# Copying the shifted values by halves of the heads, in other units, and loading the first half of the values earlier, in an attention-and-experts kernel

## The chip, the cores and the metric

The kernel runs on one core of a Trainium2 chip. A core has a matrix engine (TensorE, "PE" in the profile, with its weight loads as "PEld"), a vector engine (DVE), a scalar engine (ACT), GpSimd (POOL) and SyncE (SP), which here only issues transfers. Each engine works through its own list of instructions in order and waits on semaphores for the others. The metric is the device time of one execution in microseconds.

## The reference

Two blocks follow each other. The first is causal attention with a window of 64 positions over 8 batches, 8 heads, 576 positions and a head size of 64. The second sends each of the 4608 rows, 512 wide, to one of eight experts; a row may keep the expert of the row before it.

```python
scores = scale * np.matmul(q, k.transpose(0, 1, 3, 2))
mask = (rel >= 0) & (rel < window)          # rel = query position - key position
attn = softmax(np.where(mask, scores, -1e9))
x = np.matmul(attn, v)                      # (B, H, S, D) -> (B, S, H*D)
...
e = fresh_e if s == 0 or local_gate[b, s] < 0.5 else prev_e
h = np.maximum(x[b, s] @ w1[e], 0.0)
out[b, s] = p[e] * (h @ w2[e])
```

## The kernel before

The 4608 rows are cut into nine spans of 512 (`SC`), and the eight heads into four pairs. One span and one pair of heads, written (sc, hp) here, is a unit; there are 36 of them, and `attention` walks through them in order. For each unit `scores` (from L329) makes the transposed scores in PSUM on PE (L335), ACT takes the exponential (L351) and DVE multiplies with a 0/1 mask (L354). `values` (from L357) multiplies the result with the values on PE (L364); a column of ones beside the values gives the sum, DVE takes its reciprocal (L369) and scales the rows (L374). Scores run two units ahead of values (`LEAD`), so in the step of unit (sc, hp) PE makes first the scores of the unit two further on, and then the values of (sc, hp).

Keys are needed in blocks of 64. A query block in an even place uses the 64 keys of the block before it and its own, and these lie in other halves of the 128 partitions than for a query block in an odd place. So there are two copies of the values of a span: `va` as loaded, and `vb`, shifted by 64 positions: its lower 64 partitions are those of `va`, its upper 64 partitions are those of the chunk of 128 positions before. `shift(sc)` (from L306) makes `vb` of a span: the upper half by ACT in three copies (L311, L314, L318), the lower half by POOL in two (L312, L316). It is a generator; each `next` lets it issue the part up to the next `yield`. `shift_first` (from L320) does the same for span 0 by halves of the heads (POOL L326, ACT L327). There are three `va` and two `vb` buffers.

The steps in which the parts of `shift(sc + 1)` are issued are set at L414 to L417: for span 0 all four parts in unit (0, 3), for the later spans two parts in unit (sc, 0) and two in unit (sc, 1).

ACT, PE and SP take their instructions in the order in which the program text issues them (L179); DVE and POOL are ordered by a scheduler. What else stands in ACT's queue near the copies: for the spans 0 to 3, `turn` transposes the finished rows x of a span on PE, two pairs of heads at a time (L259), and ACT copies the result out of PSUM (L262). The first half of span sc is turned in unit (sc, 3), the second half in unit (sc + 1, 0). `gates(sc)` in unit (sc + 1, 1) multiplies this with the gate weights on PE (L273), and ACT copies the product out (L280, tile `gs`); in unit (sc + 1, 2) PE transposes `gs` (L285) and DVE sums it into the logits (L291). For the spans from 4 on, the logits come from the values directly: `gates(sc + 1)` in unit (sc, 2) (L275, L280), and `spread` in unit (sc, 3) puts them as extra columns beside `va` and `vb` (ACT L301 to L303, DVE L304). PSUM results of `values`, `turn`, `gates` and the router alternate between two banks (`bank`).

At the start SP loads in this order: keys and queries of pair 0, of pair 1, the first half of the heads' values, keys and queries of pairs 2 and 3, the second half of the values (L217; keys and queries come together, as `kq`). PE first runs 12 transposes of the identity (`warm`, L223), which compute nothing that is used, then the scores of the units (0, 0) and (0, 1), then 24 more such transposes, and then the values of (0, 0). DVE builds the second mask (L245, L248) after the mask product of (0, 1). The load of span 2 waits, by a tiny transfer on SP's queue (L213), for the first reciprocal.

After attention, `Experts` runs the experts' matrix products on the sorted rows (L1203, L1234, L1112, L1155), with weights loaded two jobs ahead into the buffers that keys and queries had.

Of the kernel before, what the change touches and what calls it, by code (L numbers as in the profile page):

```python
# [20 lines left out]
B, H, S, DH = 8, 8, 576, 64  # L21
# [3 lines left out]
WIN = 64  # L25
# [28 lines left out]
NSC = N // SC  # L54
# [95 lines left out]
def attention(ctx, tc, ring, kq, v3, v4, vt, vh, xs, lt, ok, wg, wg2, ident, rt, ex):  # L150
# [14 lines left out]
    nc = tc.nc  # L165
# [9 lines left out]
    def bank():  # L175
        ps_x.reverse()
        return ps_x[0].tile([P, 2, SC], F32, name="xo")
# [3 lines left out]
    kqs, qts, kts, vts, vas, vbs = {}, {}, {}, {}, {}, {}  # L181

    def width(sc):
        return VW if sc in GATED else VX

    def space(name, sc):
        return kp.tile([P, 4, H, width(sc)], F32, name=name, bufs=2 if name == "vb" else 3)

    def load(sc, parts):
        for part in parts:  # L190
            if part == "turned":
                t = tp.tile([P, HP * (SC + WIN)], F32, name="vtt")
                vts[sc] = main, ahead = t[:, :HP * SC], t[:, HP * SC:]
                nc.sync.dma_start(out=main, in_=vt[GATED.index(sc)].rearrange("p h x -> p (h x)"))
                if sc - 1 not in GATED:

                    nc.sync.dma_start(out=ahead, in_=vh.rearrange("p h x -> p (h x)"))
            elif isinstance(part, tuple):
                if sc not in vas:
                    vas[sc] = space("va", sc)  # L200
                src, h = v4[GATED.index(sc)] if sc in GATED else v3[sc], slice(*part)
                nc.sync.dma_start(out=vas[sc][:, :, h], in_=src[:, :, h])
            else:
                if sc not in kqs:
                    kqs[sc] = ring.tile([P, HP, 2, SC], F32, name="w")
                    kts[sc], qts[sc] = kqs[sc][:, :, 0], kqs[sc][:, :, 1]
                nc.sync.dma_start(out=kqs[sc][:, part], in_=kq[sc, :, part])
# [3 lines left out]
    def until(i, x):  # L211

        nc.sync.dma_start(out=late[:, i:i + 1], in_=x)  # L213

    pairs = slice(0, HP // 2), slice(HP // 2, HP)
    whole = (0, H)
    load(0, [slice(0, 1), slice(1, 2), (0, H // 2), pairs[1], (H // 2, H)])  # L217

    def warm(n):

        r = bank()
        for _ in range(n):
            nc.tensor.transpose(r[:, 0, :P], ident, ident)  # L223
# [16 lines left out]
    def build_mask(i):  # L240
        m = cp.tile([P, KB, 2, WIN], F32, name=f"mask{i}")
        for c in range(2):
            h = slice(c * WIN, (c + 1) * WIN)
            for par in range(2):
                nc.vector.tensor_scalar(m[h, :, par, :], colf[h], rowf[h], None, Alu.is_ge if par == c else Alu.is_lt)  # L245
        mid = MID[i]
        other = slice((1 - mid % 2) * WIN, (2 - mid % 2) * WIN)
        nc.vector.memset(m[other, mid // 2, mid % 2, :], 0.0)  # L248
        masks.append(m.rearrange("p a b q -> p (a b q)"))
# [38 lines left out]
    def logits(sc, gated):  # L288

        gt = back(*gated).rearrange("p (c h g) -> p c g h", c=4, h=HP)[:, :, :E + 1]  # L290
        nc.vector.tensor_reduce(lt[:, 4 * sc:4 * sc + 4, :], gt, axis=AX.X, op=Alu.add)  # L291
# [14 lines left out]
    def shift(sc):  # L306

        va = vas[sc]
        vb = vbs[sc] = space("vb", sc)
        w = slice(width(sc - 1))  # L310
        nc.scalar.copy(vb[WIN:, 0, :, w], vas[sc - 1][WIN:, 3])  # L311
        nc.gpsimd.tensor_copy(vb[:WIN, :2], va[:WIN, :2])  # L312
        yield
        nc.scalar.copy(vb[WIN:, 1:3], va[WIN:, :2])  # L314
        yield
        nc.gpsimd.tensor_copy(vb[:WIN, 2:], va[:WIN, 2:])  # L316
        yield
        nc.scalar.copy(vb[WIN:, 3], va[WIN:, 2])  # L318

    def shift_first(half):  # L320

        va, h = vas[0], slice(4 * half, 4 * half + 4)
        if not half:
            vbs[0] = space("vb", 0)
            nc.gpsimd.memset(vbs[0][WIN:, 0], 0.0)
        nc.gpsimd.tensor_copy(vbs[0][:WIN, :, h], va[:WIN, :, h])  # L326
        nc.scalar.copy(vbs[0][WIN:, 1:, h], va[WIN:, :3, h])  # L327

    def scores(sc, hp):  # L329
        qt, kt = qts[sc], kts[sc]  # L330
        sp = ps_s.tile([P, 2, SC], F32, name="sp")

        def one(j, c, kt, block, a, b):
            h = slice(j * DH, (j + 1) * DH)
            nc.tensor.matmul(sp[c * WIN:(c + 1) * WIN, j, a:b], lhsT=kt[h, hp, block * WIN:(block + 1) * WIN],  # L335
                             rhs=qt[h, hp, a:b], start=True, stop=True)

        for s in range(5):
            for c in range(2):
                for j in range(2):  # L340
                    if c == 0:
                        if s < 4:
                            one(j, 0, kt, 2 * s, s * P, (s + 1) * P)
                    elif s:
                        one(j, 1, kt, 2 * s - 1, s * P - WIN, min(s * P + WIN, SC))
                    elif sc:
                        one(j, 1, kts[sc - 1], KB - 1, 0, WIN)
                    else:
                        one(j, 1, kt, 1, 0, WIN)
        p = pp.tile([P, 2, SC], F32, name="p")  # L350
        nc.scalar.activation(p, sp, Act.Exp, scale=DH ** -0.5)  # L351
        a = 0 if sc == KB else (MID[sc % 2] - sc) * WIN
        m = masks[sc % 2][:, a:a + SC].rearrange("p (o x) -> p o x", o=1)
        masked.append(nc.vector.tensor_tensor(p, p, m.to_broadcast([P, 2, SC]), op=Alu.mult))  # L354
        return p
# [23 lines left out]
    masked = []  # L379
    for u in units[:LEAD]:  # L380
        ps[u] = scores(*u)
    shift_first(0)
    with tc.issue_after(masked[-1].ins):
        build_mask(1)
    warm(24)
    until(0, masks[0][:1, :1])
    load(1, [pairs[0], whole, pairs[1]])
    moves, gated, turned, old = (), None, None, None
# [17 lines left out]
    for i, (sc, hp) in enumerate(units):  # L406
        if hp == 0:
            x, g = wk.tile([P, 4, HP, 2, DH], F32, name="x"), None
            if sc in GATED:
                g = wk.tile([P, 4, HP, 2, E + 1], F32, name="g")  # L410

        if 1 < i < len(units) - LEAD:
            ps[units[i + LEAD]] = scores(*units[i + LEAD])
        if hp == (0 if sc else 3) and sc + 1 < NSC:  # L414
            moves = shift(sc + 1)
        for _ in range(2 if sc else 4):
            next(moves, None) if moves else None  # L417
        if hp == HP - 1:
            if sc + 1 in GATED:
                spread(sc + 1, gated)  # L420
            if sc not in GATED:
                turn(sc, x, 0)
                old = x
        elif sc and sc - 1 not in GATED:
            if hp == 0:
                turn(sc - 1, old, 1)
            elif hp == 1:
                turned = gates(sc - 1)
            else:
                logits(sc - 1, turned)  # L430

        if side is None and 4 * sc >= C1 and hp >= 2:
            side = rt.first(psum)
        step()
        values(sc, hp, ps.pop((sc, hp)), x, g)
        if i < 2:
            ps[units[i + LEAD]] = scores(*units[i + LEAD])
        if i == 0:
            shift_first(1)
            until(1, allr[:1, 0, 0, 0, :1])  # L440
            load(2, [pairs[0], whole, pairs[1]])
        if i == 2 * HP:
            with tc.issue_after(masked[-1].ins):
                rt.prepare()
        if hp == 2 and sc + 1 in GATED:
            gated = gates(sc + 1)
        if 0 < sc < NSC - 2 and hp in (0, 2):
            load(sc + 2, [pairs[1]] if hp else [whole, pairs[0]])
        if hp == 2 and sc + 2 in GATED:
            load(sc + 2, ["turned"])  # L450
        if (sc, hp) == (NSC - 3, 3):
            ex.jobs = [ex.weights({}, -1)]
            if side == ():
                ex.rows(ex.jobs[0], -1)
        if (sc, hp) == (NSC - 1, 0):
            ex.jobs.append(ex.weights({}, -2))
        step()
        if hp == HP - 1:
            if sc in GATED:
                nc.vector.tensor_reduce(lt[:, 4 * sc:4 * sc + 4, :], g.rearrange("p c h j e -> p c e (h j)"),  # L460
                                        axis=AX.X, op=Alu.add)
            nc.gpsimd.dma_start(out=xs[sc * SC:(sc + 1) * SC, :].rearrange("(c p) d -> p c d", p=P),
                                in_=x.rearrange("p c h j d -> p c (h j d)"))
# [899 lines left out]
```

## Time and profile before

| what | us |
|---|---|
| ten runs: median (lowest to highest) | 664.06 (662.17 to 668.14) |
| the profiled execution | 666.12 |
| its span, first to last instruction | 664.4 |
| PE busy in the span | 631.8 (95%) |
| DVE / ACT / POOL busy | 384.2 / 177.9 / 124.8 |
| matrix products of scores, L335 (72 instructions each for 36 pairs of weight load and product) | 44.8 |
| exponentials, ACT L351, 36 of them | 36.9 |

The page gives for each engine its busy time, and in its groups the idle time just before an instruction with what ended it ("<-"). "issue" there means that the instruction waited for nothing that the profile shows. A timeline line has the start, the duration, the engine, the line of the kernel, what is written from what, and in brackets the idle time before it.

### The profile page before, as it was taken

What the parts mean: (1) busy time and instruction counts of PE and PEld (TensorE: products, weight loads), DVE (VectorE), ACT (ScalarE), POOL (GpSimd) and SP (SyncE); (2) the same over time, 40 slices, a digit from 0 to 9 for tenths busy, and PEclk for the clock granted to TensorE, in tenths of its full rate; (3) what the DMA queues carried; (4) which work ended last, traced back from release to release, by engine and by line L of the source; (5) the groups of instructions that cost most, each with busy time, mean ns of one, the idle gap of its engine ahead of it and who ended that gap; (6) DMA issues with size and microseconds to landing.
All of it is one profiled execution on the core that took longest, in us unless ns stands there. A gap on an engine that the chain in (4) does not pass through costs nothing. (4 is left out here: it accounts for less than half of the span.)

```text
span 664.4 us, 15065 instructions
## 1 busy us (share of the span) xinstructions
PE 631.8 (95%) x6521; PEld 546.0 (82%) x6521; DVE 384.2 (58%) x693; ACT 177.9 (27%) x274; POOL 124.8 (19%) x128
## 2 busy tenths in 40 slices
PE   8889877989999999999999999999999999999995
PEld 7667665777777789989989998999799979997973
DVE  6665679773941168358628844863566366637310
ACT  3755645521211121203212130322131213211200
POOL 4411112311214101122113111311211120101011
PEclk9999989999999999999999999999999999999998
DMA  8989889999877967487459557755865586457540
GB/s 336 420 316 365 326 296 360 381 354 364 299 287 297 382 239 270 190 306 295 166 218 371 213 219 281 293 205 177 312 246 194 189 313 240 160 198 287 195 155 23
DMA packets 22479, 178.37 MB, mean 268 GB/s; under 512 B 3037, under 2 KB 4195, under 8 KB 11652
## 3 DMA queue, kind: packets, MB, share of 16 engines
q1 hardware_dynamic: 13588, 147.82, 59.0%
q0 software_dynamic: 8816, 29.50, 11.2%
q8 instruction: 53, 0.87, 0.5%
q14 instruction: 22, 0.18, 0.1%
HBM read 158.43 MB, written 19.40 MB: 268 GB/s over the span
## 5 line engine op out<-in xcount | busy, mean ns | idle before, releaser
L1185 POOL DMA_INDIRECT out_dram<-y,idx x36 | 39.8, 1106 | 301.6 <-DVE y L1164 142.1
L1203 PEld LDWEIGHTS hp<-xt,w 128*128 128x128 f32 (+1 forms) x1152 | 88.2, 168 | 3.4 <-issue 3.1
L1203 PE MATMUL hp<-xt,w 128*128 128x128 f32 (+1 forms) x1152 | 89.4, 252 | 0.0
L1112 PE MATMUL hp<-xs,ws 128*128 128x128 f32 x624 | 73.9, 275 | 0.0
L1112 PEld LDWEIGHTS hp<-xs,ws 128*128 128x128 f32 x624 | 71.8, 192 | 0.0
L1155 PE MATMUL hp<-ws,hs 128*128 128x256 f32 x312 | 71.6, 379 | 0.0
L1234 PE MATMUL yp<-w,h 128*128 128x512 f32 x160 | 70.9, 594 | 0.0
L1036 POOL DMA_INDIRECT xg<-xs,idx x40 | 46.2, 1156 | 114.6 <-PE tp L1061 84.1
L1155 PEld LDWEIGHTS hp<-ws,hs 128*128 128x128 f32 x312 | 59.3, 190 | 8.1
L354 DVE TENSOR_TENSOR p<-p,mask 128x1024 f32<-128x1024 f32 x36 | 46.1, 1286 | 22.6 <-ACT p L351 22.4
L1234 PEld LDWEIGHTS yp<-w,h 128*128 128x128 f32 x160 | 29.5, 190 | 32.6 <-issue 31.8
L1123 DVE TENSOR_TENSOR h<-hp,keep 128x512 f32<-128x512 f32 x39 | 26.9, 691 | 49.1 <-PE hp L1112 49.1
L364 PE MATMUL xo<-vb,p 128*64 128x74 f32 (+1 forms) x576 | 44.4, 229 | 9.2 <-DVE va L304 5.3
L364 PEld LDWEIGHTS xo<-vb,p 128*64 128x64 f32 x576 | 38.8, 138 | 17.2 <-issue 8.0
L1112 PEld LDWEIGHTS hp<-xt,w 128*128 128x128 f32 x416 | 49.3, 192 | 3.4 <-issue 2.4
L1112 PE MATMUL hp<-xt,w 128*128 128x128 f32 x416 | 51.0, 276 | 0.0
L1164 DVE SCALAR_TENSOR_TENSOR y<-hp,pw,kept 128x256 f32<-128x256 f32 x39 | 18.3, 481 | 56.2 <-issue 33.6
L351 ACT ACTIVATE p<-sp 128x1024 f32<-128x1024 f32 x36 | 36.9, 1026 | 47.9 <-PE sp L335 42.9
L1155 PE MATMUL hp<-w,h 128*128 128x256 f32 x208 | 49.5, 381 | 0.0
L335 PE MATMUL sp<-w 64*64 64x128 f32 (+1 forms) x1296 | 44.8, 278 | 3.3 <-issue 3.3
L335 PEld LDWEIGHTS sp<-w 64*64 64x64 f32 x1296 | 39.2, 143 | 10.5 <-issue 8.3
L364 PE MATMUL xo<-va,p 128*64 128x74 f32 (+1 forms) x576 | 44.5, 229 | 1.2 <-issue 1.2
(268 smaller groups left out, 898.8 us busy)
## 6 DMA issues: line engine op xcount, KB each, us to landing
w<-in_w_dram SPq DMA_DIRECT2D x54, 2048.0 KB, 8.7
w<-in_kq_dram SPq DMA_DIRECT2D x17, 1024.0 KB, 11.8
xs<-x POOLq DMA_DIRECT2D x9, 1024.0 KB, 12.0
va<-in_v_dram SPq DMA_DIRECT2D x5, 1184.0 KB, 5.4
vtt<-in_vt_dram SPq DMA_DIRECT2D x5, 1024.0 KB, 5.1
va<-in_v_dram SPq DMA_DIRECT2D x3, 1040.0 KB, 11.1
va<-in_v_dram SPq DMA_DIRECT2D x2, 520.0 KB, 7.9
w<-in_kq_dram SPq DMA_DIRECT2D x2, 512.0 KB, 4.0
```

Source lines behind the costliest of these rows:

```text
L335: nc.tensor.matmul(sp[c * WIN:(c + 1) * WIN, j, a:b], lhsT=kt[h, hp, block * WIN:(block + 1) * WIN], rhs=qt[h, hp, a:b], start=True, stop= ...
L351: nc.scalar.activation(p, sp, Act.Exp, scale=DH ** -0.5)
L354: masked.append(nc.vector.tensor_tensor(p, p, m.to_broadcast([P, 2, SC]), op=Alu.mult))
L364: nc.tensor.matmul(xo[par * WIN:(par + 1) * WIN, j, s * VW:s * VW + n], lhsT=p[:, j, b * WIN:(b + 1) * WIN], rhs=w[:, s, 2 * hp + j, :n], ...
L1036: self.nc.gpsimd.indirect_dma_start(out=x, out_offset=None, in_=self.xs[:rows, :], in_offset=bass.IndirectOffsetOnAxis(ap=idx[:, s:s + 1], ...
L1112: nc.tensor.matmul(out[:, m, :], lhsT=a[:, kk, m * P:(m + 1) * P], rhs=b[:, kk, :], start=start and m + kk == 0, stop=stop and (m, kk) == ...
L1123: nc.vector.tensor_tensor(o, x, y, op=add)
L1155: nc.tensor.matmul(out, lhsT=a[:, m, :], rhs=b[:, m, :], start=start and m == 0, stop=stop and m == FK // 2 - 1, skip_group_check=True)
L1164: nc.vector.scalar_tensor_tensor(y[i][:, j * w:(j + 1) * w], x, pw[i], y2, Alu.mult, Alu.add)
L1185: self.nc.gpsimd.indirect_dma_start(out=self.out[:, :], out_offset=bass.IndirectOffsetOnAxis(ap=st["idx"][:, s:s + 1], axis=0), in_=y, in_ ...
L1203: nc.tensor.matmul(hp[a, i, :], lhsT=st["w1"][:, kk, m * P:(m + 1) * P][:, a], rhs=st["xt"][:, kk, :n], start=(kk == 0), stop=(kk == DK - 1))
L1234: nc.tensor.matmul(yp, lhsT=st["h"][:, m, :P], rhs=st["w2"][:, m, :], start=(m == 0), stop=(m == FK - 1))
```

## The change

It has four parts. `shift` works by halves of the heads: a half is two ACT copies (one chunk from the span before, three chunks of the own span) and one POOL copy, and there are two halves. The halves of `shift(sc + 1)` are issued in units (sc, 1) and (sc, 2), those of `shift(1)` in (0, 3) and (1, 0). At the start the first half of the values is loaded ahead of the keys and queries of pair 1. `shift_first(0)` is issued between the scores of (0, 0) and those of (0, 1), and the second group of identity transposes has 4 instead of 24.

```diff
-    load(0, [slice(0, 1), slice(1, 2), (0, H // 2), pairs[1], (H // 2, H)])
+    load(0, [slice(0, 1), (0, H // 2), slice(1, 2), pairs[1], (H // 2, H)])
...
-        w = slice(width(sc - 1))
-        nc.scalar.copy(vb[WIN:, 0, :, w], vas[sc - 1][WIN:, 3])
-        nc.gpsimd.tensor_copy(vb[:WIN, :2], va[:WIN, :2])
-        yield
-        nc.scalar.copy(vb[WIN:, 1:3], va[WIN:, :2])
-        yield
-        nc.gpsimd.tensor_copy(vb[:WIN, 2:], va[:WIN, 2:])
-        yield
-        nc.scalar.copy(vb[WIN:, 3], va[WIN:, 2])
+        for half in range(2):
+            h = slice(4 * half, 4 * half + 4)
+            nc.scalar.copy(vb[WIN:, 0, h, :width(sc - 1)], vas[sc - 1][WIN:, 3, h])
+            nc.scalar.copy(vb[WIN:, 1:, h], va[WIN:, :3, h])
+            nc.gpsimd.tensor_copy(vb[:WIN, :, h], va[:WIN, :, h])
+            yield
...
     for u in units[:LEAD]:
         ps[u] = scores(*u)
-    shift_first(0)
+        if u == (0, 0):
+            shift_first(0)
...
-    warm(24)
+    warm(4)
...
-        if hp == (0 if sc else 3) and sc + 1 < NSC:
+        if hp == (1 if sc else 3) and sc + 1 < NSC:
             moves = shift(sc + 1)
-        for _ in range(2 if sc else 4):
-            next(moves, None) if moves else None
+        if (sc, hp) in ((0, 3), (1, 0)) or sc and hp in (1, 2):
+            next(moves, None)
```

In the built programs DVE and POOL have the same instructions in the same order as before (the POOL copies with another shape); PE differs by 20 transposes, ACT by the places and number of its copies (four instead of three for each of the eight shifted spans), SP by the two exchanged loads.

## The prediction

> **What bounds the kernel now.** I first cut the span into stages, as the windows view gives them (window, length, busy time of PE, PEld, DVE, ACT, POOL with counts, TensorE clock, DMA share, GB/s).
>
> ```profile
> 23.00:80.00 57.00, 47.99 (x1099) 38.61 (x1091) 33.08 (x66) 35.04 (x43) 11.86 (x13) 1.00 0.91 349
> 80.00:120.00 40.00, 31.36 (x716) 25.77 (x720) 34.96 (x111) 18.58 (x26) 7.54 (x7) 0.91 0.90 330
> 141.00:658.00 517.00, 515.13 (x3851) 448.36 (x3846) 282.62 (x449) 102.06 (x181) 87.19 (x78) 1.00 0.66 250
> ```
>
> From 141 us on PE works 515.13 of 517 us. The change touches nothing there, so whatever is won or lost in attention moves the end by as much. In attention PE has gaps: 9.0 us of the 57 in the second to fifth span. So I ask next who ends PE's gaps (times: in total, how many, longest), from 9 to 90 us:
>
> ```profile
> PE xo L364 <- DVE va L304: 3.3, 2, 2.1
> PE xo L273 <- ACT p L262: 3.0, 4, 0.8
> PE sp L335 <- issue: 2.0, 3, 1.0
> PE xo L364 <- DVE lt L291: 1.9, 4, 0.5
> PE xo L364 <- issue: 1.3, 2, 1.0
> PE xo L259 <- issue: 1.1, 1, 1.1
> ```
>
> The second line is the one that the change reaches: the gate products wait four times for ACT's copy of the turned rows. ACT's timeline around the first of them, and the PE line that waited, show why:
>
> ```profile
> 23.64 1.03 ACT L351 ACTIVATE p<-sp 128x1024 f32<-128x1024 f32 x1 [0.27 <-PE sp L335]
> 24.68 0.62 ACT L311 COPY vb<-va 64x520 f32<-64x520 f32 x1
> 26.26 1.06 ACT L314 COPY vb<-va 64x1040 f32<-64x1040 f32 x1 [0.95 <-DMA va<-in_v_dram]
> 27.34 1.01 ACT L262 COPY p<-xo 128x1024 f32<-128x1024 f32 x1
> 28.41 1.07 PE L273 MATMUL xo<-p,wgs 128*32 128x512 f32 x8 [0.79 <-ACT p L262]
> ```
>
> In unit (1, 0) two shift copies stand between the exponential and L262, and one of them waits for values still on their way. The other three gate products start at 43.09, 58.50 and 75.06, after waits of 0.66, 0.78 and 0.73, each behind an L311 and an L314.
>
> **Part 1, the shift moves behind the turn.** In the units (2, 0), (3, 0) and (4, 0) ACT now has only the exponential and L262: at 40.40 the exponential ends, L262 would end at 41.4, and the scores ahead of the gate product end at 42.4. The wait goes, with about 1 us of cover. In unit (1, 0) a half of `shift(1)` stays ahead of L262. Its price: L327 has the shape of its larger copy (780 elements a partition) and took 0.84; the smaller (260) I put on the line through 520 elements in 0.62 and 1040 in 1.05, an estimate of 0.41. So L262 ends near 24.67 + 1.25 + 1.01 = 26.9, and the scores before the gate product end at 27.6. This wait goes too. Removed: 0.79 + 0.66 + 0.78 + 0.73 = **2.96 us**.
>
> What is late next? The half moved to unit (sc, 1) now stands between the exponential and the copy L280 of the gate product. From the start of the gate product PE has 1.07 (gates) + 1.08 (values) + 1.07 (scores) = 3.2 us until it transposes that copy; ACT needs 1.03 + 1.25 + 0.59 = 2.9, and in the wider spans about 0.1 more (copies of 592 and 1184 elements took 0.68 and 1.17). Covered, by 0.2 to 0.3. In unit (sc, 2) the second half stands before L280 of the next span's gates in the same way: exponential and half take 2.3 to 2.4, values and gates on PE take 2.2 to 2.3 before L280 could begin, and at 115.56 and 100.19 ACT had been idle 3.99 and 1.93 before it. I charge 0. Per span the halves cost ACT 2 x 1.25 against 0.62 + 1.05 + 0.62, 0.2 more, in a stage where it works 35.04 of 57 us: hidden. POOL's copies keep order and number: 0.
>
> On SP's queue the load of `va` for span 3 waits for the buffer of span 0, which the second half of `shift(1)` now reads in unit (1, 0): it issues at about 25.1, not 22.68, and the two `kq` loads behind it slip from 23.06 to about 25.5. Median landing times are these (KB each, us to landing):
>
> ```profile
> w<-in_kq_dram SPq DMA_DIRECT2D x17, 1024.0 KB, 11.8
> va<-in_v_dram SPq DMA_DIRECT2D x3, 1040.0 KB, 11.1
> ```
>
> 25.9 + 11.8 = 37.7, and span 3's scores start at 45.17; SP's next instruction is at 38.41. No cost; without that cover it would be 2.4.
>
> **Part 2, the start.** The lines that matter, PE, POOL, ACT and DVE:
>
> ```profile
> 8.41 1.04 POOL L326 COPY vb<-va 64x1040 f32<-64x1040 f32 x1 [3.55 <-DMA va<-in_v_dram]
> 8.49 3.19 DVE L354 TENSOR_TENSOR p<-p,mask 128x1024 f32<-128x1024 f32 x2 [1.46 <-ACT p L351]
> 8.84 2.84 PE L223 MATMUL xo<-ident 128*128 128x128 f32 x24
> 10.06 0.84 ACT L327 COPY vb<-va 64x780 f32<-64x780 f32 x1
> 11.60 2.46 DVE L245 TENSOR_SCALAR mask<-p,rowf 64x512 f32<-64x512 f32 x4
> 19.61 0.69 DVE L374 TENSOR_TENSOR x<-xo,allr 128x512 f32<-128x512 f32 x1
> 20.43 0.98 PE L259 MATMUL xo<-ident,x 128*128 128x128 f32 x7 [1.14 <-issue]
> ```
>
> The third load of the queue released its reader at 8.41. After the change that is `kq` of pair 1, so the scores of (0, 1), which ran from about 7.1, start at 8.4. Values (0, 0) could start earlier than 11.61, since `vb` and mask product are ready near 9.7 and 20 transposes are gone: 20 x 2.84 / 24 = 2.4 us off PE. But PE is not what decides here. DVE's order is fixed: mask product of (0, 1), second mask (2.46 + 0.11), and only then the reciprocals, rows and further mask products, with hardly a gap until L374 of (0, 2) ends at 20.30, which frees the bank for values (0, 3). The scores of (0, 1) take 1.1 (full clock) to 1.8 (3.57 for two at the low clock), the exponential 1.02, the product 1.23, with small gaps: it ends at 11.85 to 12.55 against 11.68. DVE is late by 0.2 to 0.9, and L374 of (0, 2) ends at 20.5 to 21.2. Before, values (0, 3) started at 21.35 all the same, because PE stood 1.14 inside the transposes at 20.43. So I take **0**, between +0.9 (that stall comes again, after the lag) and -0.8 (no stall, 20.5 instead of 21.35).
>
> [...]
>
> **Part 3, unmarked stalls.** The "issue" stalls fall inside runs of equal instructions, as at 20.43 after one of eight. The page has a queue of the kind "instruction" with 53 packets and 0.87 MB, 16.4 KB each, and PE has 2 x 6521 instructions: one packet to about 246 of them. I read the stalls as late instruction blocks. From 9 to 141 us they make 6.0 us (1.14, 0.40, 1.00, 1.00, 0.34, 0.65, 0.20, 1.30). [...] Dropping 20 transposes, 40 instructions, moves every block edge to another place in the code, so single stalls will shrink or grow by up to 1.3; the sum could go either way. I take 0, with 1.5 both ways. The clock is a second such matter: the 0.91 of the third stage comes from two stretches at 0.50 (87.2 to 90.5 and 114.5 to 117.8), after PE had been idle for 2.1 and 2.3; after 1.99 idle at 104 there was none. One stretch costs about 1.4 (values 1.80 against 1.25, scores 1.99 against 1.12), and a small shift may add or remove one; also 0, within the same 1.5.
>
> **Sum.** -2.96 + 0 + 0 = -3.0 on a span of 664.4, that is 661.4, and 663.1 for the profiled execution's own 666.12. That execution lies 2.1 above the median, so against the median of 664.06 I say **661.1 us**.
>
> **Rivals.**
> *Block edges take the gain.* If blocks arrive when the transfers let them and not when PE is early, a stall behind a removed wait grows by that wait. Behind the waits at 28.41, 43.09 and 75.06 stand stalls of 1.00, 1.00 and 0.65 within 6.2 us; behind 58.50 stands none. What is left is 0.78: 663.3, no change. For it: the neighbours in the trace. Against it: loads are issued when PE frees buffers, so they come earlier too.
> *The copies in the new place hold the gate copy.* If a half takes long beside POOL's copies, L280 ends late and PE waits in four units (sc, 1) and five units (sc, 2). For it: POOL's own copies took 2.14 at 18.22 instead of 1.05. Against: ACT's copies ran in 0.62 and 1.05 at that very time. It decides from about 2.0 us a half on (1.25 + 0.2 spare + 0.55, as 9 x 0.55 = 5 outweighs 2.96 by 2); at doubled copies, 2.5, it costs 9 x 1.05 = 9.5 and gives 664.06 - 2.96 + 9.5 = 670.6.
> *More is won.* The stall at 20.43 and the one behind 75.06 vanish too: -0.8 and -0.65 more, 659.6.
>
> **Chances.** Forecast 0.50, block edges 0.28, copies late 0.12, more 0.10. A difference under 0.3%, 2.0 us, can hardly be told from none. About 0.07 of the forecast and all of the second case lie within it: faster 0.53, same 0.34, slower 0.13. Range 658.9 to 664.9: the forecast's 1.5 both ways, the third case and the whole second case with its own 1.5.
>
> **What would show it.** Right: no L273 wait on L262 in the four units, L311 and L314's successors after L351 in the units 1 and 2, L280 ended before L285 starts, values (0, 3) within 0.9 of 21.35, PE without gaps from about 138. Wrong: L285 waiting for L280, "issue" stalls clearly over 6 us before 141, or scores of (0, 1) much later than 8.4.

## The result and the profile after

The changed kernel is slower: 668.41 us, the median of 17 runs (664.20 to 671.31), against 663.10, the median of 62 runs of the kernel before. The ratio is 1.0074, 95% interval 1.0058 to 1.0091, about 4.9 us (the two medians as they stand differ by 5.3). The prediction said 661.1, faster. All times here are of fast runs; of the runs below a single one, of `old_warm`, was slow, and it is also the one of that kernel's profile.

The two profiled executions differ by less than the medians do: spans of 665.2 after and 664.4 before, runs of 667.0 and 666.12. The one after lies below its median, the one before above its own. So the traces serve here to see where time goes in a stage, and the runs to say how much it is.

In the changed kernel the lines have other numbers: scores L332 (were L335), values L361 (L364), exponential L348 (L351), mask product L351 (L354), reciprocal L366, rows L371, `shift` on ACT L312 and L313, on POOL L314, `shift_first` on POOL L323 and on ACT L324. L202 to L304 are as they were.

First the stages of the changed kernel, in the windows view (window, length, busy time of PE, PEld, DVE, ACT, POOL, TensorE clock, DMA share, GB/s):

```profile
23.00:80.00 57.00, 48.10 (x1059) 40.34 (x1063) 32.11 (x65) 32.70 (x43) 11.85 (x13) 0.94 0.84 315
80.00:120.00 40.00, 31.83 (x750) 25.77 (x743) 35.40 (x113) 21.88 (x32) 7.15 (x6) 0.96 0.96 356
141.00:658.00 517.00, 515.57 (x3864) 449.08 (x3862) 284.10 (x454) 102.05 (x181) 88.45 (x78) 1.00 0.66 252
```

The experts' stage is unchanged, as it should be. In the second to fifth span PE is as busy as before, 48.10 against 47.99, but not with more work: it gets through 1059 products where it got through 1099, and its clock is 0.94, no longer 1.00. Next, who ended PE's gaps from 9 to 90 us (in total, times, longest):

```profile
PE xo L285 <- ACT vb L313: 2.9, 1, 2.9
PE sp L332 <- DMA w<-in_kq_dram: 2.7, 1, 2.7
PE xo L361 <- DVE lt L291: 2.2, 4, 0.6
PE xo L361 <- DVE x L371: 2.1, 1, 2.1
PE xo L361 <- DVE va L304: 1.2, 1, 1.2
PE sp L332 <- issue: 1.1, 2, 0.7
PE xo L361 <- issue: 1.0, 2, 0.8
PE xo L361 <- DVE allr L366: 0.4, 1, 0.4
PE xo L273 <- ACT p L262: 0.2, 1, 0.2
```

The wait that the change was to remove is gone: L273 on L262, 3.0 in four waits, is 0.2. Three new ones stand above it: 2.7 for the keys of pair 1, 2.1 for the rows, and 2.9 at L285. The first two belong to the start. Its lines on PE, POOL, ACT and DVE, and behind them, from the kernel before, the same two mask products and the first POOL copy beside them:

```profile
9.80 1.66 PE L332 MATMUL sp<-w 64*64 64x128 f32 x36 [2.66 <-DMA w<-in_kq_dram]
8.51 1.92 POOL L323 COPY vb<-va 64x1040 f32<-64x1040 f32 x1 [3.64 <-DMA va<-in_v_dram]
8.47 0.84 ACT L324 COPY vb<-va 64x780 f32<-64x780 f32 x1 [0.21 <-DMA va<-in_v_dram]
11.53 1.02 ACT L348 ACTIVATE p<-sp 128x1024 f32<-128x1024 f32 x1 [2.21 <-PE sp L332]
12.58 1.23 DVE L351 TENSOR_TENSOR p<-p,mask 128x1024 f32<-128x1024 f32 x1 [3.06 <-ACT p L348]
19.17 3.70 DVE L351 TENSOR_TENSOR p<-p,mask 128x1024 f32<-128x1024 f32 x2
23.02 0.69 DVE L371 TENSOR_TENSOR x<-xo,allr 128x512 f32<-128x512 f32 x1
18.75 3.04 POOL L314 COPY vb<-va 64x1040 f32<-64x1040 f32 x2 [3.65 <-DMA va<-in_v_dram]
23.86 0.33 PE L361 MATMUL xo<-vb,p 128*64 128x65 f32 x1 [2.08 <-DVE x L371]
```

```profile
17.09 2.36 DVE L354 TENSOR_TENSOR p<-p,mask 128x1024 f32<-128x1024 f32 x2
18.22 2.14 POOL L312 COPY vb<-va 64x1040 f32<-64x1040 f32 x1 [4.85 <-DMA va<-in_v_dram]
```

The values, loaded one place earlier, are there for their reader at 8.51; one place later, in the kernel before, it was 8.41. The keys of pair 1, loaded one place later, hold the scores of (0, 1) until 9.80, from about 7.1. So the exchange delays the one and hastens nothing. DVE then goes on 2.1 later than before (the mask product of (0, 1) ends at 13.81, not 11.68), loses another 1.3 in two mask products that lie beside POOL's copies (3.70 for two; before, 2.36 with the second of them beside a copy, so the cause of the 1.3 is not shown), and frees the bank for values (0, 3) at 23.71, not 20.30. The two gaps of PE, 2.66 and 2.08, are each followed by a stretch of 3.41 us at half clock, from 10.21 and from 23.86.

The 2.9 at L285 is what the prediction had set as a sign of ACT being late. It is not that. ACT around it, and the PE line:

```profile
46.66 0.59 ACT L280 COPY gs<-xo 128x512 f32<-128x512 f32 x1
48.68 0.40 ACT L312 COPY vb<-va 64x260 f32<-64x260 f32 x1
48.99 0.83 ACT L313 COPY vb<-va 64x780 f32<-64x780 f32 x1
50.36 0.66 PE L285 MATMUL xo<-ident,gs 128*128 128x128 f32 x4 [2.88 <-ACT vb L313]
```

L285 needs `gs`, ready at 47.25, and nothing of L313; the scores before it ended at 47.5. The instruction queue had its packet at 48.07, and PE went on 2.29 later. I read this as a late instruction block: PE stands until its next instructions are there. Counted over PE's records, products and weight loads together, 1730 lie ahead of this gap. Five more gaps that end 2.2 to 2.4 us after such a packet have 1473, 1985, 2241, 2497 and 5057 ahead of them, and eight in the kernel before, 2.3 to 2.55 us after a packet, have 706, 961, 1217, 1729, 1986, 3009, 4802 and 5058. From one to the next that is a multiple of 256 within one record, so I call 256 instructions a block. The view has named the last thing that had ended before the gap.

I counted such gaps in every profile: gaps of PE over 0.15 us from 9 to 141 us that end 2.2 to 2.8 us after a packet of the instruction queue, at an edge when PE's instructions are counted by 256. "Late blocks" means their sum here and below. It is 6.0 us in eight gaps before and 6.0 in six after, one profile each. How much it can differ between two executions of one kernel: the two profiles of `move_small` below have 6.4 and 7.8.

### The profile page after: what moved, and what is told of

Its sections match the earlier page's. It is cut to its first block, busy times and chain, and to the rows that moved or that the text cites. A ratio compares the mean times of both kernels' runs of the same rounds, so it can differ in the third digit from the quotient of the medians.

```text
span 665.2 us, 15043 instructions
## 1 busy us (share of the span) xinstructions
PE 630.9 (95%) x6501; PEld 545.9 (82%) x6501; DVE 384.5 (58%) x693; ACT 178.6 (27%) x282; POOL 125.4 (19%) x128
## 5 line engine op out<-in xcount | busy, mean ns | idle before, releaser
L1034 POOL DMA_INDIRECT xg<-xs,idx x40 | 47.9, 1197 | 113.9 <-PE tp L1059 83.5
L351 DVE TENSOR_TENSOR p<-p,mask 128x1024 f32<-128x1024 f32 x36 | 46.5, 1294 | 23.8 <-ACT p L348 23.7
L361 PEld LDWEIGHTS xo<-vb,p 128*64 128x64 f32 x576 | 41.0, 145 | 21.6 <-issue 11.4
L361 PE MATMUL xo<-vb,p 128*64 128x74 f32 (+1 forms) x576 | 46.1, 236 | 13.0 <-DVE va L304 5.3
L348 ACT ACTIVATE p<-sp 128x1024 f32<-128x1024 f32 x36 | 36.8, 1024 | 57.1 <-PE sp L332 53.1
L332 PE MATMUL sp<-w 64*64 64x128 f32 (+1 forms) x1296 | 44.5, 278 | 4.8 <-DMA w<-in_kq_dram 2.7
L332 PEld LDWEIGHTS sp<-w 64*64 64x64 f32 x1296 | 38.9, 143 | 10.3 <-issue 4.4
L361 PE MATMUL xo<-va,p 128*64 128x74 f32 (+1 forms) x576 | 46.6, 237 | 0.0
## 6 DMA issues: line engine op xcount, KB each, us to landing
va<-in_v_dram SPq DMA_DIRECT2D x3, 1040.0 KB, 10.2
```

The costliest lines, as they stand in the source:

```text
L361: nc.tensor.matmul(xo[par * WIN:(par + 1) * WIN, j, s * VW:s * VW + n], lhsT=p[:, j, b * WIN:(b + 1) * WIN], rhs=w[:, s, 2 * hp + j, :n], ...
L1034: self.nc.gpsimd.indirect_dma_start(out=x, out_offset=None, in_=self.xs[:rows, :], in_offset=bass.IndirectOffsetOnAxis(ap=idx[:, s:s + 1], ...
```

## The experiments

Each ran beside the kernel before on the same chip in five rounds. In the texts on record each letter for a theory is explained beside it. "Time lost to the clock" is, here and below, one minus the mean granted clock, times the time, averaged over all runs of a kernel: 4.3 to 4.6 us for the kernel before in its five series, 7.5 for the changed one. It counts half-clock stretches after the first rise to the full clock (at 8.65 in the profile before); the low clock ahead of that is not in it. What such a lost us costs can be read from the kernel before, whose program is the same in all 130 runs of the five series: over them the time rises by 0.70 us (0.56 to 0.84) for each us lost to the clock, correlation 0.68 (an association: what else moves with the clock is in it). Differences in us between kernels are differences of their ratios times 663.

### The two parts, each alone

`move_only` is the kernel before with the new `shift` and its places, without any change of the start.

> The kernel before with the new shift alone (halves, units (sc, 1) and (sc, 2)); its start is the old one. Theory A (the start loses, the moved copies win their 3 us): no wait of the gate products on the turn copy, values (0, 3) at about 21.4 as before, 2 to 3 us faster than before. Theory B (the moved copies lose, because late instruction blocks and the gate copy hold PE): 2 to 5 us slower than before. If instruction blocks take the gain back without more: within 1 us of before.

665.10 us (12 runs) against 662.86; ratio 1.0036, interval 1.0020 to 1.0052. `start_only` is the other part: the new order of the loads, `shift_first(0)` between the scores, 4 transposes, and the old `shift`.

> The new start alone (load order, early first shift, 4 transposes), with the old shift. Theory A: scores of (0, 1) at about 9.8, values (0, 3) 2 to 3 us late, 5 to 8 us slower than before, since nothing is won at the gate products. Theory B: within 1 us of before.

665.43 us (9 runs); ratio 1.0036, interval 1.0009 to 1.0062. `move_only` came out in theory B's range, `start_only` between the two forecasts. So both parts lose, 2.4 us each, and together they make the 4.9. The moved shift loses although it does what it should. PE's waits in its profile, 9 to 90 us:

```profile
PE xo L361 <- DVE va L304: 3.3, 2, 2.1
PE sp L332 <- issue: 3.0, 3, 1.4
PE xo L361 <- DVE lt L291: 2.2, 4, 0.6
PE xo L259 <- issue: 2.0, 2, 1.4
PE xo L361 <- issue: 0.5, 1, 0.5
```

No wait for L262 at all. "issue" makes 5.5 here and made 4.4 before. Up to 141 us the late blocks are 10.2 in ten gaps, against 6.0, with this one in it; behind it PE is slower for a while, the scores from 123.36 take 1.56 for 1.12, and a product of the values takes 0.33 from 125.52 where it took 0.23 at 123.06:

```profile
122.95 0.28 PE L361 MATMUL xo<-vb,p 128*64 128x74 f32 x1 [3.58 <-issue]
```

3.0 us of gate waits went and 4.2 us of late blocks came. (These are two single executions, whose spans differ by 0.6; the 2.4 is the runs'.) The time lost to the clock rose to 5.8. In the profile of `start_only` the gate waits stand, the late blocks are 3.4, and the start shows the gap of the changed kernel (2.24 ahead of the scores of (0, 1), at 9.56); the scores behind it take 1.98, for 1.12 at the full clock.

### The changed kernel with one thing of the start put back

`old_load` has the old order of the loads, `old_warm` has `warm(24)` again.

```diff
-    load(0, [slice(0, 1), (0, H // 2), slice(1, 2), pairs[1], (H // 2, H)])
+    load(0, [slice(0, 1), slice(1, 2), (0, H // 2), pairs[1], (H // 2, H)])
```

> The changed kernel with the old order of the loads: keys and queries of pair 1 ahead of the first half of the values. The copy of the first shift still stands ahead of the exponential of (0, 1), which now waits for the values. Theory A with the late keys as the cause: PE has no gap between the scores of (0, 0) and (0, 1), the time falls by 3 to 5 us from the changed kernel, to or below that of before. If it is the missing transposes or the place of the first copy that loses: within 1 us of the changed kernel.

> The changed kernel with 24 transposes again instead of 4. If the late keys are the cause: the gap ahead of the scores of (0, 1) stays, and the time stays within 1.5 us of the changed kernel or gets longer by up to 1 us, since DVE is late anyway. If the missing transposes let the clock fall: 2 to 4 us faster than the changed kernel.

`old_load`: 666.94 us (6 runs), ratio 1.0070, interval 1.0045 to 1.0095. `old_warm`: 667.21 us (7 runs), ratio 1.0062, interval 1.0038 to 1.0086. Neither can be told from the changed kernel; the time lost to the clock is 6.3 and 6.6. In the profile of `old_load` the scores of (0, 0) and (0, 1) run without a gap and the first values start at 10.11, but the late blocks are 8.7, and it is no faster. That went against the theory that late keys are all there is, and turned the question to the late blocks.

### Other places for the block edges, and small loads

`edges_before` has 12 full and 32 small transposes for the 24 at the start of the kernel before, so the edges of its instruction blocks fall elsewhere.

```diff
-    warm(24)
+    warm(12)
+    r = bank()
+    for _ in range(32):
+        nc.tensor.transpose(r[:32, 0, :32], ident[:32, :32], ident[:32, :32])
```

> The kernel before with 12 of its 24 full warm-up transposes replaced by 32 small ones of 32 x 32: about the same TensorE time at the start, but 20 more instructions net on TensorE ahead of everything else, and so all later edges of its 256-instruction blocks fall at other places. No work is changed. Theory F (late instruction blocks set part of the time): the late stalls lie at other places than before, and the time moves by 0.5 to 3 us, in either direction: ratio somewhere from 0.996 to 1.005, and not tied to 1.000. Rival S (the copies and the start cost by themselves, edges do not matter): ratio 1.000 within 0.001.

663.13 us (12 runs) against 662.48; ratio 1.0011, interval 0.9991 to 1.0032. The late blocks lie elsewhere (4.5, of them 2.8 in one gap), the time is not told from no change: a miss for the theory in its strong form. Moving the edges by itself settles nothing.

The other three have the loads of the spans after the first cut up: keys and queries by pair and kind (256 KB), values by chunk of 128 positions, turned values by pair.

```diff
-                nc.sync.dma_start(out=vas[sc][:, :, h], in_=src[:, :, h])
+                for c in range(4) if sc else [slice(None)]:
+                    nc.sync.dma_start(out=vas[sc][:, c, h], in_=src[:, c, h])
...
-                nc.sync.dma_start(out=kqs[sc][:, part], in_=kq[sc, :, part])
+                for c, j in [(c, j) for c in range(HP)[part] for j in range(2)] if sc else [(part, slice(None))]:
+                    nc.sync.dma_start(out=kqs[sc][:, c, j], in_=kq[sc, :, c, j])
```

> The kernel before, with the loads of the spans after the first cut into small transfers (keys and queries by pair, values by chunk of 128 positions, turned values by pair). Theory F (an instruction block waits behind the data that is already in the queues of the shared DMA engines): fewer and shorter late blocks in the attention stage, 6.0 us in before down to 3 or less, and the time 1 to 3 us below before, ratio 0.996 to 0.998. Rival S: no change, or slower by the cost of more transfers, ratio 1.000 to 1.003.

> The kernel before with the shift of the spans moved behind the turn and cut by halves of the heads (as in the run that moved it alone, 1.0036), and with the loads in small transfers as in the run beside it. Theory F: the move's own gain, 2.8 us of waits, appears now: 2 to 3 us below the kernel before with small loads. Rival S (the moved copies cost more than the waits they remove): slower than the kernel before with small loads by the same 2 to 3 us as with large loads.

> The changed kernel with the loads of the spans after the first in small transfers. Theory F: faster than the changed kernel by 2 to 4 us, the start's loss (first pair of scores at 9.8, first values at 23.9) stays: ratio to before 1.000 to 1.003. Rival S: as the changed kernel, 1.0074, or above.

| kernel, all with small loads | us (runs) | ratio to before, interval | lost to the clock | late blocks |
|---|---|---|---|---|
| `before_small` | 663.62 (12) | 1.0015, 0.9991 to 1.0039 | 4.4 | 6.4 |
| `move_small` | 661.25 (12) | 0.9983, 0.9962 to 1.0005 | 3.3 | 6.4 |
| `after_small` | 665.76 (8) | 1.0058, 1.0036 to 1.0080 | 7.4 | 5.7 |

Small loads by themselves bring nothing, against theory F's forecast, and they did not lessen the late blocks, which it had as its reason. But with them the kernel with the moved shift is 2.1 us faster than the one without it, as theory F had forecast, where with large loads it was 2.4 slower (the two intervals here overlap; a second series of `move_small`, further down, has 0.9958 to 0.9989). This time neither the late blocks nor the clock's loss rose with the move. The changed kernel stays slower, between its two forecasts: the start costs 5.0 us here.

### The new start, thing by thing

Four kernels, from `move_small` and `after_small`: the new load order alone; `shift_first(0)` between the scores alone; 4 transposes alone; and the changed kernel with small loads and the old load order, which has the last two together.

> The kernel with the moved shift and the small loads (0.9983 of before), with one thing of the new start alone: the first half of the values is loaded ahead of the second pair's keys and queries. Theory K (late keys make the start's loss): the scores of (0,1) move from about 7 to about 9.5, and the time goes up by 2.5 to 4.5 us, ratio 1.002 to 1.005. Theory F (what the start loses is the lottery of the late blocks): up by less than 1.5 us, ratio below 1.0005, since 24 warm-up transposes behind the scores keep the block edges where they are.

> The kernel with the moved shift and the small loads, with one thing of the new start alone: the first copies of the shift of span 0 are issued between the scores of (0,0) and (0,1). Expected by both theories: the exponential of (0,1) goes behind a copy of 0.84 us on ScalarE that waits for the values until 8.4, so about 1 us later (9.2 instead of 7.6 at the earliest), covered by the 24 transposes for the most part: 0 to 1 us, ratio 0.998 to 1.000.

> The kernel with the moved shift and the small loads, with one thing of the new start alone: 4 warm-up transposes in place of 24 behind the first scores. TensorE comes to the values of (0,0) earlier and waits for the shifted values (about 9.9); the block edges move by 20 instructions. If 20 transposes of 0.11 us were on the path: down by up to 0.5 us; if the idle time brings a half-clock stretch: up by 1.4 us. Theory F: a move by the edges of up to 2 us in either direction. Theory K: nothing, within 0.5 us.

> The changed kernel with small loads (1.0058 of before) and the old order of the first loads; the other parts of the new start stay. Theory K (late keys make the start's loss): the time falls to that of the moved shift with small loads, 0.9983, within 0.002. Theory F: it stays above 1.003, with the loss in other late blocks or in the copies between the scores.

| added to `move_small` | us (runs) | ratio to before, interval | lost to the clock | late blocks |
|---|---|---|---|---|
| the new load order | 667.91 (9) | 1.0068, 1.0044 to 1.0091 | 5.1 | 5.9 |
| `shift_first(0)` between the scores | 662.21 (12) | 0.9988, 0.9966 to 1.0010 | 3.7 | 6.2 |
| 4 transposes for 24 | 663.43 (12) | 1.0006, 0.9986 to 1.0025 | 4.9 | 10.7 |
| the last two together | 664.60 (12) | 1.0021, 0.9996 to 1.0045 | 5.9 | 7.6 |

The exchange of the two loads is the dearest single thing, 0.0085 in the ratio to before, 5.6 us, over `move_small`; that is above theory K's 1.002 to 1.005 (the interval reaches into it), and it rules out theory F's ratio below 1.0005. PE's lines in the profile of that kernel (lines have its own numbers, L226 is `warm`):

```profile
9.73 1.99 PE L335 MATMUL sp<-w 64*64 64x128 f32 x36 [2.40 <-DMA w<-in_kq_dram]
11.64 4.46 PE L226 MATMUL xo<-ident 128*128 128x128 f32 x24
16.04 0.27 PE L364 MATMUL xo<-vb,p 128*64 128x65 f32 x1
```

The keys come as late as in the changed kernel, and PE is slow for longer: these scores take 1.99, for 1.12 at the full clock, and the 24 transposes 4.46, in `move_small` 2.84. Values (0, 0) start at 16.04, in `move_small` at 10.09. The other two edits of the start shorten this (values (0, 0) at 11.91 in `after_small`), but where the loads are not exchanged they bring nothing and seem to cost: 0.0038, 2.5 us, with intervals that overlap a little. That kernel, 1.0021, lies between theory K (0.9983, within 0.002) and theory F (above 1.003) and meets neither. With large loads the same step, from `move_only` to `old_load`, is 0.0034. The profile with 4 transposes alone shows where it may go: its late blocks are 10.7 against 6.4. Over its runs the clock's loss is higher too, 4.9 against 3.3. Neither is shown to be the cause.

### Filling the idle time

If the low clock behind PE's idle time is a good part of the loss, transposes that nobody reads should bring it back. `after_fill` has 16 of them between the scores of (0, 0) and (0, 1); `before_fill` and `move_small_fill` have 8 behind each `spread`, where PE waits up to 2.1 for L304; `after_small_fill` has both.

```diff
             shift_first(0)
+            warm(16)
...
                 spread(sc + 1, gated)
+                warm(8)
```

> The changed kernel with 16 transposes that nobody reads between the scores of (0,0) and (0,1), where TensorE waited 2.66 us for the second pair's keys. The keys come no earlier: the scores of (0,1) stay at about 9.6 to 9.8. Theory C (half-clock stretches after idle time are a good part of the loss): no half-clock stretch at 10.2, the (0,1) scores take 1.1 us instead of 1.66, and the time falls by 1 to 2.5 us, ratio 1.004 to 1.006; the time lost to a low clock, 7.5 us over the runs of the changed kernel, falls by 1.5 to 3. Rival: only the late keys and late copies count, ratio stays at 1.007 within 0.001.

> The changed kernel with small loads (1.0058), with the same 16 transposes, and 8 more behind the spread of the gates, where values wait 2.1 us for the copied gate values. Theory C: two half-clock stretches fewer, 1.5 to 3 us faster than with small loads alone, ratio 1.0015 to 1.0035. Rival: 1.005 to 1.006.

> The kernel before with 8 transposes that nobody reads behind the spread of the gates (three times in the program), where TensorE waited 1.2 to 2.1 us for the copied gate values. Theory C: the half-clock stretch at 87.2 is gone in the runs that had it, 0.5 to 1.4 us faster, ratio 0.998 to 0.999. Rival: no change, ratio 1.000, or slower by up to 0.0015 where the transposes are in the way.

> The moved shift with small loads and the old start (0.9983), with 8 transposes that nobody reads behind the spread of the gates. Theory C: 0.5 to 1.4 us faster than without them, ratio 0.996 to 0.9975. Rival: 0.998 to 0.999. It is the version that may beat both kernels.

| kernel | us (runs) | ratio to before, interval | lost to the clock |
|---|---|---|---|
| `after_fill` | 666.77 (12) | 1.0055, 1.0027 to 1.0083 | 5.4 |
| `after_small_fill` | 668.34 (9) | 1.0090, 1.0059 to 1.0121 | 3.8 |
| `before_fill` | 666.92 (12) | 1.0063, 1.0042 to 1.0083 | 3.3 |
| `move_small_fill` | 667.82 (9) | 1.0066, 1.0040 to 1.0092 | 2.9 |

The clock's loss goes down as expected, by 2.1 and 3.6 in the first two and by 1.0 and 0.4 in the others. The time falls by 1.3 in the first alone, well within the intervals, and rises by 2.1, 4.2 and 5.5 in the others. The fill was not neutral: each `warm` takes one of the two banks, and after it all later work meets the other one. PE's timeline in `before_fill` has three gaps of it:

```profile
117.19 0.28 PE L364 MATMUL xo<-vb,p 128*64 128x74 f32 x1 [1.33 <-DVE va L304]
132.44 0.28 PE L364 MATMUL xo<-vb,p 128*64 128x74 f32 x1 [1.33 <-DVE va L304]
143.09 1.13 PE L1204 MATMUL hp<-xt,w 128*128 128x128 f32 x8 [1.37 <-DVE x L374]
```

The values of (sc, 3) do not need what `spread` of the next span writes, but in the other bank they have to wait for its reader. In the kernel before none of the three waits for these.

So these four do not part the clock from the banks. `after_fill_even` was to do so: two times 8 transposes at the start, two banks, and the rotation is as it was. With it, `move_small` was run again, since it had been the best of several.

> The changed kernel with two times 8 transposes that nobody reads between the scores of (0,0) and (0,1); two banks are taken for them instead of one, so the rotation of the two banks is that of the changed kernel. Theory C (the half-clock stretch at 10.2 is part of the loss): below the run with one bank more (1.0055), at 1.003 to 1.005; the profile has no half-clock stretch before 20 and no wait of the first expert product for the rows. Rival (only the late keys count): 1.006 to 1.008, as the changed kernel.

> The kernel with the old start, the moved shift and the small loads, once more. If its lead stands: ratio 0.9965 to 0.999. If it was the best of several by luck: 0.9995 to 1.002.

`after_fill_even`: 670.88 us (6 runs) against 663.69, ratio 1.0107, interval 1.0086 to 1.0128, above both forecasts and slower still than the changed kernel (its interval, 1.0058 to 1.0091, just overlaps). `move_small` again: 662.18 us (12 runs), ratio 0.9974, interval 0.9958 to 0.9989. Its lead stands, 1.7 us; it is faster than both kernels, by 0.3% or less. In the profile of `after_fill_even` PE's waits from 9 to 141 us begin with

```profile
PE xo L361 <- issue: 7.9, 5, 2.8
PE xo L361 <- DVE va L304: 5.3, 3, 2.1
PE sp L332 <- issue: 2.6, 4, 1.3
```

and the fill did its work at its place: the scores of (0, 1) start at 9.74 as without it, but take 1.12, not 1.66. PE comes to the turn in unit (1, 0) at 24.79, 2.7 ahead of the changed kernel. Then the late blocks (11.2 in nine gaps against 6.0) take it all and more; the experts' first product starts at 145.69 against 143.26. The half-clock stretch at 10.2 is gone, but the profile's mean clock is 0.989 over its 669.0 us, 7.4 us lost, and over the six runs the time lost to the clock is 7.6, as it was in the changed kernel (7.5). So the fill moved the low clock and did not lessen it. The run shows that removing it at one place does not bring the time back; how much of the loss the low clock makes in all it cannot say.

## Why the prediction was wrong

*Part 1, the moved shift: right on the waits, wrong on the path.* The waits of L273 went from 3.0 to 0.2, ACT's copies ran in 0.41 and 0.83 at their new places, L280 was in time. SP's load of `va` slipped to 29.22, further than the 25.1 foretold, and PE waited for no later keys, so that this cost nothing holds too. What failed is the step from "the wait goes" to "the span is shorter by 2.96". Alone the move cost 2.4, with 4.2 us more of late blocks in its profile. The rival "Block edges take the gain" named late blocks and left 0.78 of the gain; the run, 2.4 slower, lies 3.2 beyond that, so the rival's price was wrong as well. That late blocks are what took the gain rests on one profile of each kernel and is not shown.

*Part 2, the start: the step that failed most.* It put the scores of (0, 1) at 8.4, because the third load had released its reader at 8.41. But that load was of values; a load of keys in its place released PE at 9.1 to 9.8 in eight profiles of kernels with the new order. So the landing time of a load was not to be read from the place in the queue. From there on each number is late: DVE 2.1 behind, not 0.2 to 0.9; the bank free at 23.71, not 20.5 to 21.2; values (0, 3) 2.5 later, not 0. That values come earlier was taken for granted and not priced; they did not (7.88 to 8.53 in all profiles, in both places). What the late keys cost in time is shown with small loads, 5.6 us where they come alone; with large loads `old_load` has them early again and is no faster, so there the loss of the start can't be put down to them alone. The 2.4 us of transposes taken off were not there to be won, as the prediction had it. Where keys come early and 4 transposes stand for 24, PE waits for the shifted values instead (1.87 in `old_load`).

*Part 3, the unmarked stalls: right as a thing, too small in its bounds.* It took 0, with 1.5 both ways, for late blocks and the clock together. In the profile of the changed kernel the late blocks did keep their total, 6.0; with 2.5 to 11.2 in the profiles of all these kernels that may be chance. The clock did not: 7.5 us lost over all runs against 4.3 to 4.6, 3.0 more. A stretch of 3.41 us at half clock loses 1.7 by that measure and cost about 1.4 by the prediction's own figures, so this would be near 2.5 of the 4.9 us; by the 0.70 for each us lost in the runs of the kernel before it would be 2.1. Both are estimates. In the move alone both went against it, 4.2 of late blocks in the profile and 1.5 of clock over the runs.

By the terms that it names, the ends of the prediction's range come to 659.6 and 664.8, not 658.9 and 664.9; nothing hangs on this.

The other two rivals are out: no half was held up on ACT (0.41 and 0.84, in the wider spans 0.44 and 0.93), and the stall at 20.43 that was to vanish for "More is won" is gone, but one of 2.88 stands at another edge.

*What stays open.* Why a packet of the instruction queue comes almost as PE enters the block before it (in the kernel before one at 88.00, the entry at 88.41), or as much as 5.5 us later (32.15 after 26.63). Counted by 256 instructions, of 20 blocks up to 141 us, 10 in the kernel before were entered within 2.75 of their packet (PE had stood at eight of these edges), and 9 in the changed kernel, the slower one. So the count alone doesn't give the time. That the packets stand behind data transfers was a guess, and no run shows it: the DMA engines are 0.84 to 0.98 busy from 23 to 141 us in the two profiles, and small loads changed what the move is worth by 4.5 us, but they did not lessen the late blocks, and no run took the data away. Nor is it shown why, with large loads, the old load order won nothing (1.0070 for 1.0074) while with small ones it won 2.5 us (1.0021 for 1.0058, intervals overlapping).

In the experts' stage no such gap was found in the two profiles: a block lasts longer there (18.9 us in the median in the kernel before, 6.4 up to 141 us), and its packet comes 3.4 to 23.1 us ahead of PE's entry, 17.9 in the median (17.2 in the changed kernel). In attention it comes 2.3 to 6.9 us ahead, 2.8 in the median, and one block cost up to 3.58 (`move_only`).

## What to carry to other kernels

An engine that stands at a late instruction block at many of its block edges (8 of 20 here, up to 141 us) need not give back a wait that is removed between them; look first what the unmarked stalls total, and price a gain as a range that reaches from below zero to the full sum. A load moved ahead must be shown to land earlier at its reader (8.51 for 8.41 here), and what it is moved past must be priced with its own reader's wait. Filler work need not be free even in idle time: here it took buffers in rotation and moved all later instructions (`before_fill`, 1.0063).

## What was not expected of the hardware

Two loads of 0.5 MB issued 0.7 us apart (at 1.27 and 2.00 in the changed kernel): exchanged, the values reached their reader at 8.51 for 8.41, the keys theirs at 9.80 for 7.1 or earlier.

A gap of about 2 us on PE led to 3.41 us at half clock in some places and not in others. The wait of 2.29 ahead of L275 did so in the kernel before (it ends at 113.96, the half clock runs from 114.46 to 117.87) and did not in the changed kernel (it ends at 117.69, the clock is 1.00 from there to 141). In the kernel before the wait of 2.10 for L304 that ends at 86.62 did so (87.15 to 90.57), and one of 1.99 that ends at 105.93 did not.

In the profiles of these two kernels each change of the clock lies a whole multiple of 3.41 us behind the first one (8.65 before, 6.80 after). Cut into stretches of 3.41 us from there, and the program's end aside, PE was busy for 1.31 and 1.12 us in the two stretches of the kernel before that end with a fall to half, and for 0.75, 1.33, 0.66 and 1.31 in the four of the changed kernel. The emptiest stretches without a fall behind them had 1.70 (before, from 104.22, with most of the wait of 1.99) and 1.75 (after, from 116.02, with most of that of 2.29). The wait of 2.29 lay whole in one stretch before (111.05 to 114.46) and across two after; what decides beyond these cases, two profiles don't show.

Sixteen transposes in idle time, after which the scores that waited there started no later than without them (9.74 and 9.80), and yet the kernel was 2.2 us slower (ratios 1.0107 and 1.0074, intervals that just overlap).
